# Decay input of a fused scan and maxout kernel: two transfers of 64 partitions for four of 32, and the other chunks' decay input behind ScalarE's table load

## Chip, cores and metric

The kernel runs on one core of one Trainium2 chip. The metric is device time in microseconds of one execution; lower is better. The profiled execution is one further run, taken with the hardware profiler.

## The reference

Two blocks follow each other. The first is a state-space scan (Mamba-2's SSD form) over x of shape 4 x 8 x 768 x 32, with decays `a` of shape 4 x 8 x 768 and B and C with a state of 16. Cut to what matters, for each batch b and head h:

```python
log_a = np.log(np.clip(a, 1e-06, 1.0))
for c in range(nc):                        # chunks of the sequence
    cum = np.cumsum(la, axis=-1)           # la: log_a of the chunk
    L = np.exp(cum[..., :, None] - cum[..., None, :]) * causal
    M = einsum('bhin,bhjn->bhij', Cc, Bc) * L
    y = einsum('bhij,bhjd->bhid', M, xc) + (Cc @ state) * np.exp(cum)[..., None]
    state = np.exp(la.sum()) * state + sum_j(B_j x_j * np.exp(cum_last - cum_j))
```

The second block takes y as 3072 tokens of 256 and computes `max(max(y @ w1, y @ w2), y @ w3) @ w_out`, with 768 columns in the middle. x, a, B, C and the output are float32; the weights are float64, and the kernel decodes them to float32 on the chip.

## The kernel before

The sequence is cut into 6 chunks of 128 tokens (`NC`, `P`), with 4 batches and 8 heads in each (32 rows, `BH`). Chunk 0 has a path of its own. Its decays come straight from the input `a`: the tile `a0` holds the 32 rows four times over, once for each group of 32 partitions, so that TensorE can work on four groups at once. The chain of chunk 0 is:

- `clip` (L284) on VectorE, logarithm (L301) on ScalarE, running sum (L306) on VectorE;
- `spread_i` and `spread_j` (L367, L379) on TensorE, which put cum_i - cum_j for every head into PSUM banks that already hold the mask (L351);
- `first_exp` (L385) on ScalarE, which makes the decay matrix `L0`, and `upper` (L389) on GpSimd.

The decays of all chunks together come as the tile `a_sb` (96 partitions, two parts of 128). They go through the same clip, logarithm and running sum, and are written to a buffer in device memory, `cums` (L1063), from which chunks 1 to 5 read their decays back, spread over the partitions (`decay_load`, L428, and `last_load`, L436).

Meanwhile B and C of chunk 0 are loaded in four row pieces each (`load_rows`, L230, tile `stage`), turned by VectorE (L239) and by TensorE (L475), and go into the scores (L561). The weights are fetched in twelve pieces of 512 KB (`fetch`, L188, tile `rb`) and decoded by ScalarE (L200, L202), VectorE (L208 to L213) and GpSimd (L220). From some 50 us on the kernel is a steady sequence of weight products on TensorE (L730, L899) with the scan of the later chunks in between.

The order on every engine is written out by hand: the pools run under a manual schedule, a string of step names gives the order of the start-up, and each engine works through its instructions in that order. Transfers are issued by two queues, SP's and, at the very start alone, ScalarE's. On SP the order is: two pieces of `a0`, four of B, four of C, two weight pieces, x of chunk 0, a third weight piece, B of chunk 1, and so on. On ScalarE it is: two pieces of `a0`, `a_sb`, then the load of the activation table (L110), which must come before the first logarithm. Each transfer counts its landing on one of eight counters, taken in turn in program order over both queues; the issue of a transfer waits until the one that used its counter before has landed.

To keep TensorE at work from the first microsecond, `fill` (L407) runs seven matmuls on a constant tile, and the mask goes into the banks (L351), before the spread needs `a0`.

Of the kernel before, what the change touches and what calls it, by code (L numbers as in the profile page):

```python
# [9 lines left out]
FP32 = mybir.dt.float32  # L10
# [9 lines left out]
def kernel(  # L20
# [20 lines left out]
    nc = tc.nc  # L41
# [3 lines left out]
    P = 128  # L45
# [4 lines left out]
    BH = NB * NH  # L50
    R = BH * NC // 2
    REP = P // BH
# [12 lines left out]
    const = ctx.enter_context(tc.tile_pool(name="const", bufs=1))  # L65
# [31 lines left out]

    a_rows = a.rearrange("b h s -> (b h) s")
    a0 = const.tile([P, P], FP32, name="a0")
    for k in range(REP):  # L100
        eng = nc.sync if k % 2 == 0 else nc.scalar
        eng.dma_start(out=a0[k * BH:(k + 1) * BH], in_=a_rows[:, 0:P])

    a_sb = const.tile([R, 2, P], FP32, name="a_sb")
    nc.scalar.dma_start(
        out=a_sb,
        in_=a_rows.rearrange("r (c i) -> (r c) i", i=P).rearrange("(w r) i -> r w i", w=2))

    tabs = list(get_activation_tables(nc.m.arch).keys())
    nc.scalar.add_instruction(  # L110
# [1 line left out]
            name=nc.get_next_instruction_name(),  # L112
# [2 lines left out]
            outs=[],  # L115
        )
    )

    blocks = {c: {} for c in range(NC)}
    sources = {"B": (B, N), "C": (C, N), "x": (x, D)}  # L120
# [113 lines left out]
    def turn_rows(j, name):  # L234
# [27 lines left out]
        out=mask, in_=mask, pattern=[[1, P]], compare_op=ALU.is_ge, fill=MASKED,  # L262
# [3 lines left out]
        out=pick, in_=ident.rearrange("p (r k) -> p k r", k=BH), op=ALU.add, axis=AX.X)  # L266
    npick = const.tile([P, BH], FP32, name="npick")
    nc.vector.tensor_scalar(
        out=npick, in0=pick, scalar1=-1.0, scalar2=None, op0=ALU.mult)
# [4 lines left out]
        out=hsel, in_=hsel, pattern=[[-N, NH]], compare_op=ALU.is_ge, fill=0.0,  # L274
        base=0, channel_multiplier=1)
    nc.gpsimd.affine_select(
        out=hsel, in_=hsel, pattern=[[N, NH]], compare_op=ALU.is_ge, fill=0.0,
# [3 lines left out]
        out=parity, in_=hsel.rearrange("p (r g) -> p g r", g=2), op=ALU.add, axis=AX.X)  # L281
# [1081 lines left out]
```

## Time and profile before

| | |
|---|---|
| median of 3 runs | 259.57 us (257.83, 259.57, 259.68) |
| profiled execution, its own time | 257.81 us |
| span from the first to the last instruction | 256.1 us |
| TensorE (PE) matmul busy | 246.0 us, 96% |
| VectorE (DVE), ScalarE (ACT), GpSimd (POOL) busy | 172.6, 114.6, 112.6 us |
| TensorE busy in slices of 6.4 us | 8, 5, 8, 8 tenths in the first four, 9 or more from there to the last but one |
| transfers | 28.16 MB, mean 110 GB/s |

The busy share is an average over stages with different limits, so a change at the start is to be read from the first microseconds: from the timeline, which gives for each group of instructions the start, the length, the engine, the line, the tiles, and in brackets how long the engine had been idle before it and what ended that idle time; and from the chain, which is followed back from the last instruction and lists, for each stretch of time, what the end was waiting for. SPq and ACTq are the queues of SyncE and ScalarE that issue transfers; an issue's own length is given there, and the time from issue to landing in the list of transfers.

### The profile page before, as it was taken

The numbers are of one execution on the slowest core, as the hardware profiler recorded it, in microseconds if no ns is written. First come the engines' busy times: TensorE is split into PE (matmuls) and PEld (weight loads), VectorE is DVE, ScalarE is ACT, GpSimd is POOL, SyncE is SP. The second block draws the span as 40 slices with busy tenths as digits, with TensorE's granted clock in tenths as the row PEclk, the third lists the DMA queues.
The fourth block names the chain that finished last, engine by engine and source line by source line (L and its number), as shares of the span: only waits on it lengthen the run. The fifth ranks groups of instructions, "written<-read, shape, count | busy, mean of one in ns | idle before, by whom it ended". The sixth has DMA issues, their size and how long they took to land.

```text
span 256.1 us, 5661 instructions
## 1 busy us (share of the span) xinstructions
PE 246.0 (96%) x2168; PEld 206.3 (81%) x2168; DVE 172.6 (67%) x360; ACT 114.6 (45%) x310; POOL 112.6 (44%) x148
## 2 busy tenths in 40 slices
PE   8588999999999999999999999999999999999994
PEld 4456644587888888988899898898889899999994
DVE  5599987957845466588566688567877746655641
ACT  3778698943293656535164434354431211111010
POOL 2177674976949834661171470363230404134000
PEclk9999999999999999999999999999999999999999
DMA  3999959998996813977304835501000001001002
GB/s 107 240 169 386 283 131 273 148 215 195 198 260 87 122 34 77 259 117 113 57 0 120 247 79 94 82 3 41 3 16 27 3 3 41 0 3 41 1 24 101
DMA packets 85371, 28.16 MB, mean 110 GB/s; under 512 B 55392, under 2 KB 82016, under 8 KB 85344
## 3 DMA queue, kind: packets, MB, share of 16 engines
q1 hardware_dynamic: 84752, 27.40, 49.3%
q8 instruction: 17, 0.28, 0.5%
q10 hardware_dynamic: 592, 0.39, 0.5%
q14 instruction: 10, 0.08, 0.1%
HBM read 24.54 MB, written 3.24 MB: 109 GB/s over the span
## 4 chain that ended last, share of the span: by engine, by line
PE 83%; POOL 5%; DVE 3%; issue 2%; ACT 2%; SPq 2%; DMA 2%; POOLq 0%; DVEq 0%
PE o L899 25%; PE sumB L730 20%; PE sumA L730 16%; PE o L973 5%; PE s L561 4%; PE y L597 4%; PE up L669 4%; PE fold L835 2%; PE y L584 2%; DMA rb<-in_moe_w_dram 2%; SPq L230 1%; POOL w L220 1%; POOL L L1046 1%; POOL L L389 1%; PE A L524 1%
## 5 line engine op out<-in xcount | busy, mean ns | idle before, releaser
L447 ACT ACTIVATE L<-L,ncums 128x128 f32<-128x128 f32 x160 | 49.9, 395 | 5.9 <-POOL L L440 5.9
L730 PE MATMUL sumA<-yT,w 128*128 128x256 f32 x120 | 36.7, 388 | 0.0
L858 POOL TENSOR_TENSOR rb<-h 128x256 f32<-128x256 f32 x16 | 11.7, 729 | 56.6 <-DVE h L805 55.9
L730 PE MATMUL sumB<-yT,rb 128*128 128x256 f32 x120 | 35.9, 381 | 0.3 <-DVE m L770 0.3
L758 ACT COPY eu<-sumA 128x256 f32<-128x256 f32 x30 | 11.2, 372 | 55.5 <-PE sumA L730 55.5
L569 DVE TENSOR_TENSOR L<-s,L 128x512 f32<-128x512 f32 x46 | 29.4, 682 | 6.6 <-PE s L561 4.5
L730 PEld LDWEIGHTS sumB<-yT,rb 128*128 128x128 f32 x120 | 22.5, 190 | 4.0 <-issue 0.7
L440 POOL TENSOR_SCALAR_AFFINE_SELECT L<-L 128x1024 f32<-128x1024 f32 x20 | 22.2, 1130 | 7.2 <-DMA L<-cums 7.2
L730 PEld LDWEIGHTS sumA<-yT,w 128*128 128x128 f32 x120 | 19.5, 191 | 3.7 <-DVE rb L792 1.0
L669 PE MATMUL up<-yT,w 128*128 128x256 f32 (+1 forms) x64 | 21.9, 493 | 0.4 <-DVE w L705 0.2
L768 DVE TENSOR_TENSOR eu<-sumA,eu 128x256 f32<-128x256 f32 x30 | 12.7, 423 | 14.0 <-ACT eu L758 14.0
L858 POOL TENSOR_TENSOR w<-h 128x256 f32<-128x256 f32 x12 | 8.8, 730 | 27.9 <-DVE h L805 27.5
L220 POOL TENSOR_TENSOR w<-w_u,w_r 128x512 uint32<-128x512 uint32 x9 | 13.1, 1452 | 14.8 <-DVE w_u L213 14.0
L561 PE MATMUL s<-CT,BT 32*128 32x256 f32 x192 | 15.9, 404 | 2.6 <-ACT CT L498 1.8
L669 PEld LDWEIGHTS up<-yT,w 128*128 128x128 f32 x64 | 11.7, 189 | 7.9 <-issue 4.9
L899 PE MATMUL o<-rb,h 128*128 128x128 f32 x120 | 18.0, 275 | 0.0
L899 PE MATMUL o<-wo,h 128*128 128x128 f32 x120 | 18.0, 275 | 0.0
L730 PE MATMUL sumA<-ys,rb 128*128 128x256 f32 x60 | 17.8, 379 | 0.0
L730 PE MATMUL sumB<-ys,w 128*128 128x256 f32 x60 | 17.8, 379 | 0.0
L730 PE MATMUL sumB<-ys,rb 128*128 128x256 f32 x60 | 17.8, 379 | 0.0
L792 DVE TENSOR_TENSOR m<-sumB,eu 128x512 f32<-128x512 f32 x15 | 10.3, 688 | 9.5 <-PE sumB L730 9.5
L561 PEld LDWEIGHTS s<-CT,BT 32*128 32x128 f32 x192 | 10.0, 184 | 8.2 <-ACT L L385 2.2
(151 smaller groups left out, 522.1 us busy)
## 6 DMA issues: line engine op xcount, KB each, us to landing
L<-cums SPq DMA_DIRECT2D x10, 1024.0 KB, 9.3
rb<-in_moe_w_dram SPq DMA_DIRECT2D x9, 512.0 KB, 6.1
raw_x<-in_x_dram SPq DMA_DIRECT2D x6, 512.0 KB, 7.1
out_dram<-ob SPq DMA_DIRECT2D x10, 256.0 KB, 2.3
rb<-in_moe_w_out_dram SPq DMA_DIRECT2D x3, 512.0 KB, 7.4
E<-cums SPq DMA_DIRECT2D x40, 32.0 KB, 4.3
raw_B<-in_B_dram SPq DMA_DIRECT2D x4, 256.0 KB, 5.2
raw_C<-in_C_dram SPq DMA_DIRECT2D x24, 32.0 KB, 1.9
```

Source lines behind the costliest of these rows:

```text
L220: nc.gpsimd.tensor_tensor(out=dst.bitcast(U32), in0=v.rearrange("p (k f) -> p k f", k=2), in1=r.rearrange("p (k f) -> p k f", k=2), op=ALU ...
L440: nc.gpsimd.affine_select(out=Ls[c][:, b], in_=Ls[c][:, b], pattern=[[0, NH], [1, P]], compare_op=ALU.is_ge, fill=MASKED, base=0, channel_ ...
L447: nc.scalar.activation(L[:, b, h], L[:, b, h], AF.Exp, bias=ncum[c][:, b * NH + h:b * NH + h + 1], scale=1.0)
L561: nc.tensor.matmul(out=s[:, i].rearrange("j g i -> j (g i)"), lhsT=st["BT"][rows, b], rhs=st["CT"][rows, b].rearrange("p g i -> p (g i)"), ...
L569: nc.vector.tensor_tensor(out=M, in0=s, in1=M, op=ALU.mult)
L669: nc.tensor.matmul(out=bank[:, a:b], lhsT=w_sb[i][:, k, f * P:(f + 1) * P], rhs=yT[0][:, k, a:b], start=(k == 0), stop=(k == KD - 1), skip ...
L730: nc.tensor.matmul(out=bank[:, half], lhsT=left(p, k), rhs=sides[c][p], start=(first and half == 0), stop=True, skip_group_check=True)
L758: nc.scalar.copy(out=eu[:, 0], in_=units[c, k][0][:, 0])
L768: nc.vector.tensor_tensor(out=eu[:, 1], in0=A[:, 1], in1=eu[:, 0], op=ALU.add)
L858: eng.tensor_tensor(out=to, in0=a1, in1=a0, op=ALU.subtract)
L899: nc.tensor.matmul(out=o[SLOT[p]], lhsT=x[:, u * P:(u + 1) * P], rhs=right(p, pair), start=(p in opens and pair == 0), stop=True, skip_gro ...
L973: nc.tensor.matmul(out=o[:, i], lhsT=one, rhs=two, start=(f == 0), stop=(f == NF + KD - 1), skip_group_check=True)
```

## The change

The four loads of `a0` (32 partitions each, two on SP's queue and two on ScalarE's) become two (64 partitions each, one on each queue). Each reads the 32 rows twice, through a source pattern whose first dimension has step 0. And the load of `a_sb` on ScalarE's queue moves from ahead of the table load to behind it. Nothing else is touched; the order of everything else on each engine stays.

```diff
     a_rows = a.rearrange("b h s -> (b h) s")
     a0 = const.tile([P, P], FP32, name="a0")
-    for k in range(REP):
-        eng = nc.sync if k % 2 == 0 else nc.scalar
-        eng.dma_start(out=a0[k * BH:(k + 1) * BH], in_=a_rows[:, 0:P])
-
-    a_sb = const.tile([R, 2, P], FP32, name="a_sb")
-    nc.scalar.dma_start(
-        out=a_sb,
-        in_=a_rows.rearrange("r (c i) -> (r c) i", i=P).rearrange("(w r) i -> r w i", w=2))
+    for k, eng in enumerate((nc.sync, nc.scalar)):
+        eng.dma_start(
+            out=a0[2 * k * BH:2 * (k + 1) * BH],
+            in_=a_rows[:, 0:P].unsqueeze(0).to_broadcast([2, BH, P]))
 
     tabs = list(get_activation_tables(nc.m.arch).keys())
     nc.scalar.add_instruction(
...
     )
+
+    a_sb = const.tile([R, 2, P], FP32, name="a_sb")
+    nc.scalar.dma_start(
+        out=a_sb,
+        in_=a_rows.rearrange("r (c i) -> (r c) i", i=P).rearrange("(w r) i -> r w i", w=2))
```

## The prediction

> **What bounds the kernel now.** I read the engine shares of the page first, then the chain of work that ended last, then the timeline of the first 13 us, where everything that the diff touches lies. TensorE is busy for 96% of the 256.1 us span and holds most of the chain:
>
> ```profile
> PE 246.0 (96%) x2168; PEld 206.3 (81%) x2168; DVE 172.6 (67%) x360; ACT 114.6 (45%) x310; POOL 112.6 (44%) x148
> ...
> PE 83%; POOL 5%; DVE 3%; issue 2%; ACT 2%; SPq 2%; DMA 2%; POOLq 0%; DVEq 0%
> ```
>
> An edit at the start can only move the whole kernel earlier or later; it takes no matmul away. So the question is what the chain goes through at the start. From its view in order of time (start, length, what):
>
> ```profile
> 0.80 0.38 SPq L102
> ...
> 4.94 0.42 SPq L230
> 5.36 0.04 issue
> 5.41 4.02 DMA rb<-in_moe_w_dram
> 9.43 0.02 issue
> 9.45 0.66 ACT w_u L200
> ...
> 11.14 0.60 ACT CT L498
> 11.74 0.04 issue
> 11.78 1.40 PE s L561 x15
> ```
>
> The start is bound by SP's queue: ten transfers are issued one behind the other (two of a0, four of B, four of C), and only then the first piece of w2, which lands at 9.43 and lets ScalarE go on. The decay input a0 isn't on this chain. The timeline shows why (start, length, engine, line; in brackets the idle time before and what ended it):
>
> ```profile
> 0.80 0.89 ACTq L102 DMA_DIRECT2D a<-in_a_dram  x2
> 0.80 0.85 SPq L102 DMA_DIRECT2D a<-in_a_dram  x2
> 1.70 1.80 SPq L230 DMA_DIRECT2D stage<-in_B_dram  x4
> 1.73 0.45 ACTq L105 DMA_DIRECT2D a_sb<-in_a_dram  x1
> 2.20 1.28 ACT L110 ACT_TABLE_LOAD   x1 [2.20 <-issue]
> 3.27 0.23 DVE L284 TENSOR_SCALAR a<-a 128x128 f32<-128x128 f32 x1 [0.61 <-DMA a<-in_a_dram]
> 3.44 1.06 PE L351 MATMUL spread<-mask,ident 128*128 128x512 bf16 x2
> 4.30 0.29 DVE L284 TENSOR_SCALAR a_sb<-a_sb 96x256 f32<-96x256 f32 x1
> 4.43 1.26 PE L367 MATMUL spread<-a,pick 32*128 32x128 f32 x32
> 6.58 1.58 ACT L385 ACTIVATE L<-spread 128x512 f32<-128x512 f32 x3 [1.54 <-PE spread L379]
> 9.45 0.66 ACT L200 ACTIVATE w_u<-rb 128x512 f32<-128x512 f32 x1 [1.29 <-DMA rb<-in_moe_w_dram]
> ```
>
> VectorE's clip waits for a0 (3.27). Clip, logarithm, running sum, spread (L367, L379) and the three exponentials (L385) follow without a gap worth naming and end at 8.16. Then ScalarE stands idle for 1.29 us until the weight piece is there. So a0's chain has 1.29 us of slack, and SP's queue has none.
>
> **The change part by part.**
>
> *One issue less on each queue.* SP's eight loads of B and C start 0.463 us apart ((4.94 - 1.70)/7). With one a0 issue instead of two, everything behind it on SP could go 0.46 us earlier: B from 1.24, C from 3.08, the first weight piece at 4.95 instead of 5.41. This step alone would be worth -0.46, on the path.
>
> *When a0 lands.* The issues to landing now:
>
> ```profile
> a_sb<-in_a_dram ACTq DMA_DIRECT2D x1, 96.0 KB, 2.6
> ...
> a<-in_a_dram ACTq DMA_DIRECT2D x2, 16.0 KB, 1.8
> a<-in_a_dram SPq DMA_DIRECT2D x2, 16.0 KB, 1.6
> ```
>
> Each a0 transfer of today has 32 rows of 512 bytes and completes in 16 parts, two rows a part. As built, the new one has the source pattern 2 x 32 x 128 with step 0 in the outermost place, against 64 rows on the other side. No transfer in this trace has an outermost dimension below 16, so no row prices it, and I bound it. Upper end of speed: the spread stays at 16, and a0 lands like a first transfer today, 0.80 + 1.8 = 2.6; the clip goes to about 2.8, 0.47 earlier. Lower end: the spread follows the outermost dimension, so that two DMA engines carry all the rows, and the same two for both queues: 64 rows each instead of two. The packet records give 27 ns for a 512-byte packet (median); 62 more make 1.67 us, so a0 lands at 2.5 + 1.67 = 4.2. With 20 ns (413 GB/s, the best rate in the first 25 us, over 16 engines) it is 3.7; with 60 ns (L<-cums, 1024 KB in 9.3 us, 7.7 without the 1.6 of a short transfer, 128 rows an engine) 6.2. I take 4.2: the one thing that differs from every priced transfer is that outermost 2. [...]
>
> *What the late a0 does to VectorE, ScalarE, TensorE.* The clip now starts 0.2 after the last landing; at 4.4 it is 1.13 later than now. Behind it on VectorE wait the running sum, the clip of a_sb and the two transposes of B and C; ScalarE's logarithm and TensorE's spread wait with them. The exponentials would end at 9.29. The weight piece today lands at 9.43, so 1.13 is hidden by the 1.29. Without this cover it would cost all of 1.13.
>
> *What it does to SP's queue.* In both kernels as built, the transfers count on eight completion counters in turn, and an issue waits until the transfer eight places before has landed. Today the fourth load of B and the first three of C wait for the four a0 transfers, which have landed by then (3.07, against issues from 3.08 on). Changed, the second and third loads of C are the ones that wait for a0. The second would be due at 3.55 and now can't go before a0 is there: 4.2. Behind it are two C loads and the weight piece: 4.2 + 0.05 + 3 x 0.463 = 5.6 instead of 5.41. So the 0.46 is taken back and 0.2 is lost; break-even is a landing at 4.0. What is late next is the weight piece, at 9.6; ScalarE's decode, CT (L498) and the scores (L561) move with it, and beyond them the transfers that keep the DMA engines 90% busy until some 45 us.
>
> *Table load and a_sb.* The load of 1.28 us goes up to 1.27 and ends at 2.55; it now ends at 3.48, just ahead of the logarithm at 3.53, so it stops being a second limit; with a late a0 that gains nothing. The a_sb issue goes between 1.27 (if ScalarE's queue runs ahead of the load) and 2.55 (if it doesn't); with its 2.6 us it lands at 3.9 to 5.2. It is needed behind a0's running sum, 4.3 today and 5.4 then: nothing. Were a0 early, it could make VectorE wait to 5.2 and the transposes of B and C move by 0.9, in front of scores that start only at 11.78: still nothing. In the counters, the second weight piece waits for a_sb, due 6.1: nothing.
>
> **Sum.** +0.2 (SP behind a0's counter) + 0 (a0's chain, hidden) + 0 (table, a_sb) = +0.2 us on the profiled execution's 257.81, that is 258.0. The runs shown are 257.83, 259.57 and 259.68, so the profiled one lies with the fastest and 1.76 below the median; carried over to the median, 259.8.
>
> **The rivals.**
>
> *The spread stays at 16 engines.* Then a0 lands at 2.6, no counter holds SP, and the weight piece lands 0.46 earlier; a0's chain, 0.47 earlier, stays inside its slack. Profiled: 257.35, at the median 259.1. For it: all transfers of the trace complete in 16 parts. Against it: the outermost 2. To be faster by 1% (2.6 us), five times this gain would be needed, and SP's queue has no more to give.
>
> *TensorE's clock (slower).* The matmuls that fill TensorE's time at the start end at 4.50, and L367 begins at 4.43: no gap. The clock records give full rate from 4.65 on; until then it was slower (L351: 1024 bf16 columns in 1.06 us, where L730 later does 1024 fp32 columns in 0.86). With a0 at 4.2, L367 starts at 5.56 and TensorE idles for 1.06 us just where the rate went up after 3.53 us of unbroken work (1.12 to 4.65). If the gap makes the rate wait for another such stretch, half the work of 3.53 us is lost, 1.76, of which 0.16 of slack is left to hide any: +1.6 over the +0.2, 259.6 profiled; with a second stretch up to +3.4, 261.4. It decides from the point at which a0's chain begins behind the fill, a landing after 3.3. [...] For it: unbroken work until the rate rises, and runs in two groups 1.8 us apart, as if the start sometimes missed it already. Against it: until 4.65 only 0.15 us would be missing. At the median, where the late group may already be what is counted, some 260 to 262.5.
>
> *Two engines, and slower than 27 ns a row.* At 60 ns a0 lands at 6.2: SP is 2.2 late, a0's chain 3.1 less 1.29 = 1.8; the larger counts, +2.2: 260.0 profiled, 261.8 at the median.
>
> **How the numbers follow.** Forecast 0.45; 16 engines 0.20; clock 0.25; slow rows 0.10. A measurement of this kernel tells about 1% from no change. Slower by over 1% is 262.2: part of the clock's and of the slow rows' share, 0.20. Faster by over 1% is 257.0; even with 16 engines and the fast group the time is 257.35, so 0.06. Within 1%: 0.74. The range goes from 257.4 (16 engines, fast group) to 262.0 (clock, one stretch and part of the next).
>
> **What would show it.** Right: a0's issue to landing near 3.4 us for both halves; the clip at about 4.4; a wait of some 0.6 us on SP ahead of the second C load; the first weight piece issued near 5.6; table load from 1.27; no idle time on ScalarE longer than 0.5 before L200. A landing at 2.6 and the weight piece issued at 4.95 would prove the spread wrong; a full clock later than 4.65 in the changed profile, with L367 and L379 at half speed, would be the clock. The forecast is wrong if the scores (L561) start over 1 us away from 12.0.

## The result and the profile after

The changed kernel takes 259.95 us (median of 18 runs, 259.36 to 261.38). The kernel before, measured again beside it, takes 258.12 us (18 runs, 257.78 to 259.93). Compared on the same chip the ratio is 1.0051, with a 95% interval of 1.0033 to 1.0069: slower by half a per cent, less than the 1% of the prediction's bound but clear of its own interval. The profiled execution took 259.91 us, with a span of 258.2 where it was 256.1.

The page after still shows a kernel bound by TensorE, but the chain now begins with a0 and no longer holds SP's queue:

```profile
PE 248.3 (96%) x2168; PEld 208.3 (81%) x2168; DVE 172.0 (67%) x360; ACT 114.5 (44%) x310; POOL 112.5 (44%) x148
...
PE 86%; POOL 3%; ACT 3%; DVE 3%; issue 2%; DMA 2%; POOLq 0%; DVEq 0%
```

From the chain in order of time (start, length, what), with line numbers one higher than before:

```profile
0.80 4.42 DMA a<-in_a_dram
...
6.33 2.09 PE spread L368 x32
8.42 1.35 PE spread L380 x7
9.77 1.56 ACT L L386 x3
11.32 0.55 ACT w_u L201
...
13.54 1.40 PE s L562 x15
```

The same in the timeline, with the idle time of each engine and what ended it:

```profile
0.80 0.70 SPq L101 DMA_DIRECT2D a<-in_a_dram  x1
0.80 1.14 ACTq L101 DMA_DIRECT2D a<-in_a_dram  x1
...
1.98 1.28 ACT L106 ACT_TABLE_LOAD   x1 [1.98 <-issue]
2.01 0.37 ACTq L116 DMA_DIRECT2D a_sb<-in_a_dram  x1
...
3.39 3.09 SPq L231 DMA_DIRECT2D stage<-in_C_dram  x4
...
5.24 0.23 DVE L285 TENSOR_SCALAR a<-a 128x128 f32<-128x128 f32 x1 [2.60 <-DMA a<-in_a_dram]
...
6.33 2.09 PE L368 MATMUL spread<-a,pick 32*128 32x128 f32 x32 [1.83 <-DVE a L307]
6.52 0.94 SPq L189 DMA_DIRECT2D rb<-in_moe_w_dram  x2
...
8.19 1.52 PE L380 MATMUL spread<-npick,a 32*128 32x512 f32 x8
...
11.19 0.68 ACT L201 ACTIVATE w_u<-rb 128x512 f32<-128x512 f32 x1
```

The clip of a0 starts at 5.24 instead of 3.27 (+1.97). TensorE idles for 1.83 us ahead of the spread, and the spread's two parts take 2.09 and 1.52 us instead of 1.26 and 1.03. So the exponentials begin at 9.75 instead of 6.58, 3.17 later. The 1.29 us for which ScalarE used to wait for the weights are gone, and its decode starts at 11.19 instead of 9.45. The scores follow 1.76 late (13.54 against 11.78), and the span ends 2.1 late. The clock records give TensorE's full rate from 9.19 us instead of 4.65, and half rate once more from 19.43 to 22.84.

SP was held up as well, by a0's counter:

```profile
SPq L231 <- DMA a<-in_a_dram: 1.4, 1, 1.4
```

Its first weight piece is issued at 6.52 instead of 5.41 and lands, by the landing records, at 10.95, while ScalarE works on the exponentials: this wait stands beside the other, and the other ends last, by 0.24 us.

### The profile page after: what moved, and what is told of

It is laid out like the page before. It is cut to its first block, busy times and chain, and to the rows that moved or that the text cites. A ratio compares the mean times of both kernels' runs of the same rounds, so it can differ in the third digit from the quotient of the medians.

```text
span 258.2 us, 5657 instructions
## 1 busy us (share of the span) xinstructions
PE 248.3 (96%) x2168; PEld 208.3 (81%) x2168; DVE 172.0 (67%) x360; ACT 114.5 (44%) x310; POOL 112.5 (44%) x148
## 4 chain that ended last, share of the span: by engine, by line
PE 86%; POOL 3%; ACT 3%; DVE 3%; issue 2%; DMA 2%; POOLq 0%; DVEq 0%
PE o L900 24%; PE sumB L731 20%; PE sumA L731 16%; PE o L974 5%; PE s L562 5%; PE y L598 4%; PE up L670 3%; PE fold L836 2%; PE y L585 2%; DMA a<-in_a_dram 2%; PE y L611 1%; ACT L L386 1%; PE trB L476 1%; PE spread L368 1%; PE A L525 1%
## 5 line engine op out<-in xcount | busy, mean ns | idle before, releaser
L221 POOL TENSOR_TENSOR w<-w_u,w_r 128x512 uint32<-128x512 uint32 x9 | 13.0, 1449 | 17.1 <-ACT L L386 11.6
```

The costliest lines, as they stand in the source:

```text
L221: nc.gpsimd.tensor_tensor(out=dst.bitcast(U32), in0=v.rearrange("p (k f) -> p k f", k=2), in1=r.rearrange("p (k f) -> p k f", k=2), op=ALU ...
```

## Experiments

All are compared with the kernel before on the same chip; its median was 258.28 to 258.39 us there.

**Where a0's lateness comes from.** The first experiment keeps everything of the change but the source pattern.

```diff
         eng.dma_start(
             out=a0[2 * k * BH:2 * (k + 1) * BH],
-            in_=a_rows[:, 0:P].unsqueeze(0).to_broadcast([2, BH, P]))
+            in_=a.rearrange("b h (c i) -> (b h c) i", i=P)[0:2 * BH])
```

> The changed kernel with one thing altered: each a0 transfer of 64 rows reads 64 plain consecutive rows instead of 32 rows twice (so chunk 0 gets other decays: what is left out is the replication), with the same count, bytes, queues and order. Theory A, the outermost dimension of 2 confines the transfer to two DMA engines and that alone makes a0 late: with an outermost dimension of 64 all 16 counts of the landing come from transfers, the clip of a0 starts at 3.0 to 3.3 us instead of 5.24, SP waits for nothing and issues the first weight piece at 4.9 to 5.2 instead of 6.52, and the time is 257.4 to 258.2. Rival B, a transfer of 64 rows is itself late, or its longer issue (0.70 and 1.14 us against 0.4) is: the clip stays near 5 us and the time near 259.9. Rival C, a_sb behind the table load costs: the clip is early, but the time stays above 259.

Measured: 258.47 us (10 runs), ratio 0.9993 (0.9962 to 1.0023). The source's outermost dimension is 64 here. All 16 landing counts come from the transfers, and the clip is nearly where it was before:

```profile
a<-in_a_dram SPq DMA_DIRECT2D x1, 32.0 KB, 2.2
a<-in_a_dram ACTq DMA_DIRECT2D x1, 32.0 KB, 2.5
```

```profile
0.80 0.57 SPq L101 DMA_DIRECT2D a<-in_a_dram  x1
...
3.35 0.23 DVE L285 TENSOR_SCALAR a<-a 128x128 f32<-128x128 f32 x1 [0.69 <-DMA a<-in_a_dram]
...
5.28 0.94 SPq L189 DMA_DIRECT2D rb<-in_moe_w_dram  x2
```

Theory A holds, B and C fall. But the time is not below before, where 257.4 to 258.2 was expected: an issue of 64 rows takes 0.57 us, not 0.42, the four issues of B take 1.95 us instead of 1.80, and the first weight piece goes out only 0.13 us earlier. Even where the spread is right, the merge gives nothing that these runs can tell from zero.

**The merge alone.** a_sb is put back ahead of the table load.

```diff
+    a_sb = const.tile([R, 2, P], FP32, name="a_sb")
+    nc.scalar.dma_start(out=a_sb, ...)
+
     tabs = list(get_activation_tables(nc.m.arch).keys())
...
-    a_sb = const.tile([R, 2, P], FP32, name="a_sb")
-    nc.scalar.dma_start(out=a_sb, ...)
```

> The first part of the change alone: two broadcast transfers for a0, and a_sb again ahead of the table load. Theory A (two DMA engines carry a0's rows): the clip at 5.0 to 5.4 us, SP held ahead of the second C load, time 259.5 to 260.3 as for the whole change. Rival C (the move of a_sb is what costs): the time goes back to 258.1.

Measured: 259.98 us, ratio 1.0052 (1.0025 to 1.0079), the clip at 5.54, SP held for 1.7 us. The whole loss is in the first part of the change. The clip is 0.14 past the expected range's end.

**The table load alone.** Four a0 transfers as before, a_sb behind the table load.

```diff
-    for k, eng in enumerate((nc.sync, nc.scalar)):
-        eng.dma_start(
-            out=a0[2 * k * BH:2 * (k + 1) * BH],
-            in_=a_rows[:, 0:P].unsqueeze(0).to_broadcast([2, BH, P]))
+    for k in range(REP):
+        eng = nc.sync if k % 2 == 0 else nc.scalar
+        eng.dma_start(out=a0[k * BH:(k + 1) * BH], in_=a_rows[:, 0:P])
```

> The second part of the change alone: four a0 transfers as before, a_sb behind the table load. In the changed kernel a_sb's issue began 0.04 us after the table load had begun, so ScalarE's queue runs ahead of the load. Theory A: the table load starts at 1.75 instead of 2.20, a_sb is issued at 1.8, the clip stays at 3.27, the scores at 11.7 to 11.8, and the time is that of before within 0.2%. Rival C (the move costs, because a_sb waits for the table): a_sb issued after 3.0, landed after 5.5, time above 258.8.

Measured: 258.42 us, ratio 0.9994 (0.9962 to 1.0027); the table load at 1.73, a_sb issued at 1.76, the scores at 11.75. The move costs nothing and brings nothing.

**Four engines for two.** a0 as one transfer of 4 x 32 rows.

```diff
-    for k, eng in enumerate((nc.sync, nc.scalar)):
-        eng.dma_start(
-            out=a0[2 * k * BH:2 * (k + 1) * BH],
-            in_=a_rows[:, 0:P].unsqueeze(0).to_broadcast([2, BH, P]))
+    nc.sync.dma_start(
+        out=a0, in_=a_rows[:, 0:P].unsqueeze(0).to_broadcast([REP, BH, P]))
```

> a0 as a single broadcast transfer of 4 x 32 rows on SP; nothing on ScalarE's queue ahead of the table load, and a_sb behind it. Theory A: the outermost dimension is 4, so 4 of the 16 landing counts come from transfers, four engines carry 32 rows each with no second queue beside them; a0 lands at 3.0 to 3.6 us, the clip starts at 3.2 to 3.8, SP isn't held up for long, and the time lies between before and after, 257.6 to 258.8. Rival B (what costs is the size of one transfer and its issue): 128 rows are worse than 64, the clip starts after 5.5 and the time is above 260.

Measured: 258.93 us, ratio 1.0000 (0.9973 to 1.0027).

```profile
0.80 0.73 SPq L100 DMA_DIRECT2D a<-in_a_dram  x1
...
3.96 0.23 DVE L283 TENSOR_SCALAR a<-a 128x128 f32<-128x128 f32 x1 [1.31 <-DMA a<-in_a_dram]
```

In the trace's landing records this transfer has four counts with data, from 3.80 to 3.94 us; each of the changed kernel's two has two (5.01 and 5.02, 5.21 and 5.22); each of the kernel before's has sixteen. So the outermost dimension of the source sets here how many engines carry a0, and twice the rows in one transfer land 1.3 us sooner on twice the engines. The transfer of four copies repeats its rows too and is far less late, so the repeated reading as such isn't what delays a0; no run repeats the rows behind a larger outermost dimension. The clip came 0.16 later than the expected range, the median 0.13 above it.

**TensorE kept at work until a0 is there.** The changed kernel with nine more fill matmuls.

```diff
     fill(0, 5)
     spread_mask(0)
-    fill(1, 2)
+    fill(1, 11)
     spread_mask(1)
```

> The changed kernel with nine more fill matmuls (0.21 us each, 1.9 us) on TensorE ahead of the second mask, so that it has work until a0 is there. Theory A with two waits side by side (a0's chain ends at 11.33, the first weight piece lands at 10.95): the clock is at full rate by 6.3 us, L368 and L380 take 1.3 and 1.0 us instead of 2.09 and 1.52, the exponentials end near 10.1, but ScalarE then waits for the weight piece to 10.95, so the scores start only 0.3 to 0.4 us earlier and the time is 259.5. Rival D, the late clock is the whole loss: the scores start at 12.3 or earlier and the time is 258.1 to 258.7.

Measured: 259.27 us (258.62 to 260.34), ratio 1.0023 (0.9992 to 1.0054). In the profiled execution the clock rises at 6.96 and the spread is fast again:

```profile
6.35 1.44 PE L368 MATMUL spread<-a,pick 32*128 32x128 f32 x32
7.62 1.03 PE L380 MATMUL spread<-npick,a 32*128 32x512 f32 x8
```

The scores start at 12.47, 1.07 earlier than in the changed kernel, 0.69 later than before. The spread begins when it did there (6.35 against 6.33), so the 1.07 is the faster spread and not an earlier a0. The late clock is thus a part of the loss and not all of it. Theory A's second half failed here: ScalarE did not wait for the weight piece. In this execution ScalarE's half of a0 had landed at 3.77 already, SP was held for 0.3 us instead of 1.4, and the piece went out at 5.68. Had it landed at 10.95, as in the changed kernel, ScalarE would have waited for it, and less of the 1.07 would be left. SP's second C load counts behind ScalarE's half of a0 and its third behind SP's own; the landing of ScalarE's half moved between 3.77 and 5.52 us from kernel to kernel, and the runs don't show why.

**The late clock without a late a0.** The kernel before with two of its seven fills.

```diff
-    fill(0, 5)
+    fill(0, 1)
     spread_mask(0)
-    fill(1, 2)
+    fill(1, 1)
```

> The kernel before with 2 of its 7 fill matmuls (one ahead of each mask), so that TensorE's first work has gaps of some 0.5 us while a0 lands as before. It measures the clock's share by itself. Theory D (a gap in the first 3.5 us of work puts the release off): full rate not before 8 us, L368 and L380's counterparts L367 and L379 take 2.0 and 1.5 to 1.7 us, the exponentials end 1.2 us later but inside their slack, the scores start at 11.8 to 12.2, and the time is 258.1 to 258.6: without the late a0 the late clock is nearly hidden. Rival E (a late clock always costs its full 1.2 us): 259.3 or more with scores at 13.

Measured: 258.41 us (258.00 to 258.98), ratio 0.9980 (0.9953 to 1.0007).

```profile
4.54 2.09 PE L367 MATMUL spread<-a,pick 32*128 32x128 f32 x32 [0.53 <-DVE a L306]
6.42 1.93 PE L379 MATMUL spread<-npick,a 32*128 32x512 f32 x8
```

The clock rises only at 12.62. The first part of the spread takes what it takes in the changed kernel (2.09 us), the second longer (1.93 against 1.52). The median is as expected for theory D, and the rival's 259.3 isn't reached by any run. But the moment at which the clock rises is on record for the profiled execution alone (its mean granted clock is 1.000, so the mean leaves out the time before the rise). That execution took 258.89 us, and its scores start at 12.71, later than the 12.2 expected and 0.93 later than before. So in the median of the ten runs less fill costs next to nothing; that the clock was as late in all of them isn't shown. A late clock and a late a0 delay the same exponentials, so they draw on the same 1.29 us.

**The clock lost after the start.** The medians above carry a scatter: in the kernel before, 12 of 31 runs of the first comparison lie at 259.48 to 260.51, the rest at 257.80 to 258.64. The mean granted clock goes with it: 0.992 to 1.000 in the lower group, 0.98 to 0.987 in the upper but for one run at 0.993. The loss of the changed kernel isn't of this kind: six of its 18 runs have a mean clock of 1.000 and lie at 259.48 to 260.19. The experiment fills TensorE's idle time ahead of the scores.

```diff
         spread_banks(2, (pin("sumA"), pin("ffn")))
         spread_banks(3, 2 * [pin("sumB")])
+        fill(2, 8)
         spread_i((2, 3), True)
```

> The kernel before with eight more fill matmuls (0.86 us at full rate) on TensorE between the transpose of C and the second spread (L367), where it otherwise idles for 1.8 us ahead of the scores. In the runs of before, those near 258.0 have lost no clock or one stretch of 3.41 us after the release, those near 259.5 two, those near 260.4 three. Theory F (the upper group comes from clock lost in TensorE's idle time between 10 and 22 us): with this gap filled the share of runs above 259 falls from 12 of 31 to under 1 in 5, the rest stay at 258.0. Rival G (the groups come from elsewhere, a transfer or an order): the share stays near 12 of 31.

Measured: 258.10 us (12 runs, 257.84 to 258.68), ratio 0.9975 (0.9950 to 0.9999). No run is in the upper group, against 12 of 35 of the kernel before in the same comparison. Theory F holds: the upper group goes with lost clock, and work in the gap takes it away.

**What is left of the change's loss when no clock is lost.** The changed kernel with both fills.

```diff
-    fill(1, 2)
+    fill(1, 11)
...
         spread_banks(3, 2 * [pin("sumB")])
+        fill(2, 8)
```

> The changed kernel with nine more fill matmuls ahead of the second mask and eight ahead of the second spread, so that it loses no clock at the start and only the late a0 is left. Theory A (two causes: the late a0 by itself, some 0.7 us after the 1.29 us of slack, and the late clock, some 1.2): 258.6 to 259.0 with few runs above 259.3. Rival D (the loss is the clock alone): 258.1, as the kernel before with its gap filled. Rival H (the loss is the late a0 alone): 259.8.

Measured: 258.76 us (258.36 to 259.78), ratio 1.0006 (0.9980 to 1.0032). The runs lie in two groups, seven at 258.36 to 258.86 and five at 259.30 to 259.78. Four of the five have a mean clock of 1.000, so it isn't clock lost after the rise; where their time goes wasn't followed up. The profiled execution (258.36) is one of the first group, with the clock up from 4.79 us on:

```profile
4.76 0.23 DVE L285 TENSOR_SCALAR a<-a 128x128 f32<-128x128 f32 x1 [2.11 <-DMA a<-in_a_dram]
...
9.74 0.67 ACT L201 ACTIVATE w_u<-rb 128x512 f32<-128x512 f32 x1 [0.28 <-DMA rb<-in_moe_w_dram]
```

The clip is 1.49 later than before, and yet ScalarE waits for the weight piece: with no clock lost, the slack hides this much. The scores start at 12.09, and at 12.00 in the profiled execution of the kernel before with its gap filled (258.28). In the medians there are 0.66 us against that kernel (258.10) and 1.19 against the changed one (259.95), as theory A has it. But the 1.19 isn't the clock's alone: in the profiled execution ScalarE's half of a0 had landed at 3.87, the clip came 0.48 earlier than in the changed kernel, and SP was held for 0.2 us instead of 1.4. How the loss is shared out between the late a0, the late clock and SP's wait stays open.

**SP's queue, with a0 on 16 engines.** One a0 transfer on SP, three on ScalarE's queue, a_sb behind the table load.

```diff
-    for k, eng in enumerate((nc.sync, nc.scalar)):
-        eng.dma_start(
-            out=a0[2 * k * BH:2 * (k + 1) * BH],
-            in_=a_rows[:, 0:P].unsqueeze(0).to_broadcast([2, BH, P]))
+    for k in range(REP):
+        eng = nc.sync if k == 0 else nc.scalar
+        eng.dma_start(out=a0[k * BH:(k + 1) * BH], in_=a_rows[:, 0:P])
```

> Four a0 transfers of 32 rows with 16 landing counts each, but one on SP and three on ScalarE's queue, and a_sb behind the table load. This has the shorter SP queue that the change was priced with, without its two DMA engines. Theory A (SP's queue sets the start, a0 has 1.29 us of slack): B issued from 1.24, the first weight piece at 4.95 (0.46 earlier), a0 complete at 3.5 and its clip at 3.7, the scores at 11.3 to 11.4, and the runs without lost clock at 257.5 to 257.7 instead of 258.0; median 257.6 to 258.2. Rival D (the clock decides): the gap of 0.3 us on TensorE before L367 makes the clock come later, the scores stay at 11.7 or later and the median rises to 259.

Measured: 258.66 us, ratio 0.9971 (0.9943 to 0.9999). The runs fall between the theories: five lie at 257.52 to 258.15 and six at 258.60 to 258.77. (One of the twelve took 643.74 us, with nothing in the records to say why.) In the profiled one (258.77) the weight piece goes out at 4.94, as priced, but the clip starts at 4.11, not 3.7, the gap on TensorE is 0.69 us, and the clock rises at 8.71 only; the scores start at 12.73. No run of the lower group was profiled.

**Both together.** The same with three more fills ahead of L367 and eight ahead of the second spread.

```diff
     spread_mask(0)
-    fill(1, 2)
+    fill(1, 5)
     spread_mask(1)
...
         spread_banks(3, 2 * [pin("sumB")])
+        fill(2, 8)
```

> The version that the runs so far point to: one a0 transfer on SP and three on ScalarE's queue, a_sb behind the table load, three more fill matmuls ahead of the second mask (so that TensorE works until L367, which started at 5.19 there) and eight ahead of the second spread. Theory (SP's queue sets the start, as long as TensorE's clock is at full rate): scores at 11.3 to 11.6, all runs at 257.4 to 258.0, none above 258.5; median 257.6, faster than before by 0.2 to 0.3%. Rival (the fill only moves the release of the clock about): the runs stay split as without the fills, with half of them at 258.6 to 258.8.

Measured: 257.73 us (12 runs, 257.49 to 258.05), ratio 0.9953 (0.9932 to 0.9975): faster than the kernel before, in the median also than the changed one, and the split is gone. The scores start at 11.89, later than the 11.3 to 11.6 expected, in a profiled execution (258.05) in which the clock rose at 7.00 and was halved again from 17.24 to 20.65. The scores thus start no earlier than before (11.78), and which part of this version makes it the faster one isn't told apart. Its chain is almost all TensorE's own from the second microsecond on:

```profile
1.12 1.25 PE spread L407 x5
...
5.18 2.02 PE spread L367 x32
...
11.89 1.40 PE s L561 x15
```

## Why the prediction was right, and where it wasn't

- *Two engines for a0: right, and sized too small.* The landing was put at 4.2 and came at 5.0 and 5.2. The 27 ns a row held (the packet records of the changed kernel show both queues' rows taking turns, two of the one and two of the other in 47 ns); what the sum left out is that the new issues take 0.70 and 1.14 us, not 0.42, and that the first B load and a_sb use the same two engines at the same time: of the first B load's sixteen counts fourteen are there at 3.49, the last two at 5.42 and 5.54, and of a_sb's sixteen fourteen at 4.75, the last two at 6.09 and 6.12. What each of these adds wasn't measured. That an outermost 2 leaves a0 to two engines was the author's estimate when the sum took it, for no row of the kernel before prices it; the landing counts, 2 for the pattern of 2 and 4 for that of 4, bear it out. Two transfers for four brought nothing that can be told from zero where all 16 engines carry them (0.9993, 0.9962 to 1.0023).
- *SP held by a0's counter: the mechanism was right, the size and the place were not.* The wait was put at some 0.6 and was 1.4; the weight piece was put at 5.6 and went out at 6.52. It was to set the end by +0.2, and it didn't: the piece had landed 0.24 us before ScalarE turned to it.
- *a0's chain hidden in 1.29 us of slack: wrong.* This is the step that failed: the sum has +0 for it. A landing at 5.2 makes the clip 1.97 late, which is past the slack by itself, and the clock adds 1.20 (3.17 - 1.97) in the spread.
- *The clock, given as the slower rival with +1.6 on top: this is what happened in the profiled execution.* The prediction had 259.6 for it, the profiled execution took 259.91. The parts were others, though: 0.2 on SP's queue and 1.6 of clock with a0's own lateness hidden were forecast, and the trace has 1.97 of late a0 and 1.20 of clock, less the slack. Making TensorE work through the gap took 0.7 us off the median (259.95 to 259.27), both fills together 1.19; in the profiled executions of both the weight piece went out earlier as well. The +1.6 rested on an estimate too, that the rate waits for another 3.53 us of unbroken work: in the changed kernel it rose 2.86 us after the spread began (6.33 to 9.19). What sets the moment isn't shown: in four kernels whose TensorE starts alike up to 4.4 us the first rise lies at 4.66 (the kernel before), 4.87 (the table load alone), 4.98 (64 plain rows) and 6.03 us (the gap filled). The half-rate stretch within the changed kernel's span lasts 3.413 us, and the full-rate stretches last 3 and 69 times as long there (10.24 and 235.52 us) and 74 times in the kernel before (252.59).
- *Its own signs.* Scores over 1 us away from 12.0 were to show the forecast wrong, and they start at 13.54. Of the times that were to show it right none came: the halves of a0 took 4.2 and 4.4 us to land, not 3.4, and the clip, SP's wait, the first weight piece and the table load (from 1.98 us, not 1.27) were all off. The sign named for the clock came: full rate from 9.19 us, and a spread of 2.09 and 1.52 us.
- *Table load and a_sb at nothing: right.* The issue ran 0.03 us behind the start of the load, and the move alone measures 0.9994.
- *The number.* 259.8 was forecast and 259.95 measured, and that they lie so close is luck, for the road to it was off at two places that cancel: the effect was put at +0.2 and was +1.8 between the medians (+1.3 by the ratio), and it was carried over to a median of 259.57 from three runs, of which two lie in the upper group, the one that goes with lost clock; eighteen runs put it at 258.12. Carried over to the profiled execution's group, the same sum gave 258.0, nearly 2 us too low. That the effect would stay within 1% came out.

## What to carry to other kernels

Before two transfers are merged through a broadcast pattern, look at the outermost dimension: here a leading step of 0 with few copies left the transfer to as many DMA engines (two copies landed in 2 counts, at 5.0 and 5.2 us, four copies in 4, by 3.94, and the plain 32 rows of before in 16, by 3.07), and what counted behind it, on the other queue too, waited with it (SP's second C load 1.4 us for ScalarE's half). A slack that the profile shows is one sum for all that draws on it: here a late transfer and the late clock that came of it were added up against the same 1.29 us. And TensorE's idle time in the first 20 us had a price of its own: filling one gap with idle matmuls did as much by the ratio (0.9975) as the best rearrangement of the loads (0.9971), and the two together, with three more fills, did the most (0.9953).

## What the hardware showed that I had not expected

- The issue of a transfer took longer where few engines carried it: 0.70 and 1.14 us for 64 rows on two, 0.73 for 128 rows on four, 0.57 for 64 rows on sixteen, 0.38 to 0.44 for 32 rows on sixteen.
- The clock was halved again for one stretch of 3.41 us (19.43 to 22.84 in the changed kernel), or for two (11.80 to 15.21 and 18.63 to 22.04 with 64 plain rows), while TensorE was far from idle: the stretch before the loss in the changed kernel has 2.62 us of matmuls in 3.41 (77%), while the kernel before had 1.73 us in one such stretch (51%) and lost nothing. In the changed kernel the longest gap between two matmuls of that stretch is 0.79 us. What the busy share must be to keep the rate isn't told by these records, and stays open.
- The fills at two places, 11 matmuls of 0.1 to 0.2 us that compute nothing, together with a 3 to 1 split of a0, are worth 0.47% of a 258 us kernel.
